# Two channels in one table product: 40 rows by 66 columns, with tables split by the channel's parity

## The chip, the cores and the metric

The kernel runs on one core of a Trainium2 chip. The metric is the device time of one execution in microseconds (us), the span of the core. A program is executed several times, and medians are quoted with the lowest and highest.

## The reference, cut to what matters

The result has two halves that are independent. The first is a local dilated attention (projection, logits, softmax, weighted sum, output projection). The second is a long convolution whose kernel K is made from 192 complex modes for each of 640 channels:

```python
logdA = dt * A
P = jnp.exp(logdA[:, :, None] * l[None, None, :])        # 640 channels, 192 modes, 2048 positions
K = jnp.einsum("dn,dnl,dn->dl", Cc, P, dB).real           # the kernel of the convolution
...
Yf = Uf * Kf                                              # convolution by FFT
y = irfft(Yf)[..., :L] + u * Dskip
```

The change touches only how K is made.

## The kernel before

The powers of a position l = a + 8 b are a product of two powers, so K of one channel is a matrix product over the modes: a table X (20 values of a) by a table Y (33 values of b). Five groups of 128 channels are worked through. The tables have modes on the partitions and keep the channels innermost, so that VectorE can make a table of many channels with one instruction:

```python
self.X = tp.tile([128, 20, 2, CW], bf16, name="Xtab", tag="Xtab", bufs=2)   # CW = 192 columns
self.Y = tp.tile([128, NB, 2, CW], bf16, name="Ytab", tag="Ytab")           # NB = 33
```

The price is that TensorE reads one channel's operands with a stride of 2 x 192 x 2 = 768 bytes: a round of four products takes 69 ns. One channel takes four small matmuls (real and imaginary part, 128 and 64 modes), and four channels g lie side by side in the four 32-column tiles of the array:

```python
for part in range(4):
    for i in range(8):
        for g in range(4):
            o = ps[32 * g:32 * g + 20, i, :]
            if part < 2:
                col = 32 * g + t0 + i
                MM(o, lhsT=X[:, :, part, col], rhs=Y[:, :, part, col], start=False, stop=False,
                   tile_position=(0, 32 * g), skip_group_check=True)
            else:
                ...          # the same with 64 rows, X[hb:hb + 64, ...]
nc.scalar.copy(out=Kd[:, q // 2, :, 8 * (q % 2):8 * (q % 2) + 8], in_=ps[:].rearrange("p t b -> p b t"))
```

Then `spread` multiplies the result Kd by 0/1 matrices that put each position where the FFT wants it. The order of the instructions of each engine is written down in the kernel as a text (`kgen00:129` means 129 matmuls of the first piece of the first table product), and the engines keep to it.

The softmax here doesn't subtract the row's maximum and nothing guards it: scores larger than these inputs give would overflow.

Of the kernel before, what the change touches and what calls it, by code (L numbers as in the profile page):

```python
# [17 lines left out]
NCH = 5  # L18
# [30 lines left out]
def sel_consts_np():  # L49
# [9 lines left out]
    def add(Wm):  # L59
        full = np.zeros((128, 32), np.float32)  # L60
        for g in range(4):
            full[32 * g:32 * g + 32, 8 * g:8 * g + 8] = Wm
        for i, m in enumerate(mats):
            if np.array_equal(m, full):
                return i
        mats.append(full)
        return len(mats) - 1
# [24 lines left out]
    return np.stack(mats, 1), plan  # L92
# [35 lines left out]
def att_consts_np():  # L128
# [11 lines left out]
prep:30 weights:15 k0:2 weights:15 k0:2 weights:15 k0:5 weights:15 k0:16 q0:25 v0:25 k1:25 q1:25 v1:25 k2:25 q2:16 kgen00:129 q2:9 kgen01 kgen02  # L140
kgen03:129 kgen02:128 kgen01:128 v2:25 k3:10 logits0:4 k3:2 logits0:4 k3:6 logits0:4 k3:7 q3:10 logits0:8 q3:15 logits0:4 v3:10 kgen10:33 kgen11:33
kgen12 kgen13:129 logits0:4 kgen10:64 logits0:8 v3:4 logits0:4 v3:6 kgen10:32 v3:5 logits0:4 kgen11:96 kgen12:96 av0:32 kgen12:32 av0:48 u0:8 av0:5
u0:2 av0:8 u0:2 av0:9 u0:2 av0:9 u0:2 av0:17 spec:20 av0 spec:12 av0:31 spec:32 out0:4 spec out0:3 spec:31 logits1:4 out0:2 spec out0 spec:16 out0:2
spec:15 out0:3 logits1:2 u1:8 logits1:2 out0:2 u1:2 out0:2 u1:2 out0 u1:2 logits1:4 u1:2 out0:2 spread0:8 out0:2 spread0:8 logits1:2 spread0:20
logits1:2 out0 logits1:4 spread0:8 logits1:4 out0:2 spread0:4 out0:2 spread0:2 out0 spread0:2 logits1:4 spec0:32 logits1:4 spec0 out0:4 spec0:16
out0:3 spec0:16 out0:2 spec0:15 out0 spec0:48 inv0:57 kgen20:129 inv0:7 logits1:8 kgen21 kgen22 kgen23:33 u2:2 logits1:2 kgen23:32 u2:2 logits1:2
kgen23:64 u2:2 kgen22:32 u2:2 kgen22:32 u2:4 kgen22:64 u2:4 kgen21:128 spread1:36 av1:6 spread1:8 av1:5 spread1:2 av1:8 spread1:2 av1:9 spread1:2
av1:9 spread1:2 av1:27 spec1:49 av1:15 spec1:16 av1 spec1:63 inv1:64 kgen30 kgen31:33 kgen30:32 kgen31:96 kgen30:96 kgen32 kgen33 u3:2 kgen33:32 u3:2
kgen33:32 u3:2 kgen33:32 u3:4 kgen33:32 kgen32:32 u3:6 kgen32:32 spread2:16 kgen32:32 spread2:20 kgen32:32 av1:21 spread2:8 av1:5 spread2:2 av1:8
spread2:4 av1:2 spread2:2 av1:12 spec2:6 logits2:4 spec2:26 av1:8 spec2 av1:19 spec2:16 av1:5 logits2:4 spec2:31 out1:2 logits2:4 spec2 out1:2  # L150
spec2:16 out1 spec2:15 out1:2 spec2 out1:3 spec2:15 out1:20 inv2:32 out1:7 inv2:25 kgen40:33 inv2:5 logits2:4 inv2:2 out1:2 kgen40:96 logits2:4 out1
logits2:4 kgen41 kgen42 kgen43 u4:2 kgen43:64 u4:2 kgen43:32 u4:2 kgen43:32 logits2:6 u4:2 logits2:2 u4:2 logits2:4 kgen42:32 u4:4 logits2:4 kgen42:32
u4:2 spread3:8 logits2:2 kgen42:32 spread3:8 logits2:2 spread3:12 kgen42:32 spread3:8 kgen41:32 spread3:6 kgen41:32 spread3:2 kgen41:32 spread3:6
av2:15 spread3:2 av2:33 kgen41:32 spec3:32 av2:8 spec3 av2:8 spec3:95 av2:43 inv3:32 av2:21 inv3:25 spread4:16 inv3:4 spread4:12 inv3 spread4:8 inv3:2
av2:16 spread4:16 av2:16 spec4:32 logits3:4 out2:2 spec4 logits3:2 spec4:16 logits3:2 out2:2 spec4:16 logits3:4 spec4:15 out2 spec4 logits3:4 spec4:16
out2:2 spec4:15 logits3:4 spec4 out2:2 spec4:15 logits3:4 out2:20 inv4:32 out2 logits3:4 out2:5 inv4:25 last00:18 inv4:7 logits3:12 out2:5 last01
logits3:2 last01:8 logits3:2 last01 last02 last01:8 last02:17 last03 av3:32 last03:9 last04 last03:8 av3:17 last04:17 av3:37 last05 av3:39 last05:17
av3:35 last06:10 out3:10 last06:8 out3:10 last07 out3:10 last07:17 last10:34 last11:17 out3:10 last11:17 last12:34 last13:34
""",
    mybir.EngineType.Activation: """  # L160
prep:11 am0:2 prep am0:9 weights:2 gens0:13 weights gens0:4 weights gens0:4 k0 gens0 mag0:3 k0 mag0:3 k0 mag0:2 k0 mag0:3 k0 mag0:2 q0 mag0:3 am1:11
gens1:5 q0:3 gens1 q0 v0:3 gens1 v0:2 gens1:2 k1:2 gens1 k1 gens1 k1 gens1 k1 gens1 q1 gens1 q1 gens1 q1 gens1 q1 gens1 q1 v1 gens1:2 v1 gens1 v1
gens1 v1:2 k2:2 gens1:2 k2:2 mag1:5 k2 mag1:3 q2:2 mag1:8 q2 kgen00 q2:2 kgen03 kgen02 kgen01 v2:5 k3:5 q3:5 mag2:16 kgen13 v3:2 logits0:2 v3:2 kgen10
v3 logits0:2 kgen11 kgen12 av0:2 u0:8 av0:2 spec:4 av0:2 spec:4 out0 spec:4 out0 spec:4 out0 u1:7 spread0:4 u1 out0 spread0:8 out0:2 spec0:6 out0
spec0:10 mag3:14 inv0:4 mag3:2 inv0:3 out0 kgen20 inv0 logits1:2 u2:2 logits1:2 kgen23 u2:4 kgen22 u2:2 kgen21 spread1:12 av1:2 spec1:16 mag4:8 inv1:7
mag4 inv1 mag4:7 kgen31 kgen30 u3:5 kgen33 u3:3 spread2:4 kgen32 spread2:8 av1:2 spec2:6 av1 spec2:4 av1 spec2:4 out1 spec2:2 out1:5 inv2:4 out1
inv2:4 kgen40 out1 u4:3 kgen43 u4:4 logits2:2 u4 spread3:2 logits2 spread3 logits2 spread3 kgen42 spread3:8 kgen41 spec3:16 av2:2 inv3:4 av2:2 inv3:3
spread4:4 inv3 spread4:8 av2:2 spec4:10 out2 spec4:6 out2:3 inv4:2 out2 inv4:2 out2:2 inv4:3 last00:2 inv4 logits3:2 out2 last01 logits3:2 last01
last02:2 av3:2 last03:2 av3:2 last04:2 av3:2 out3 last05:2 out3:3 last06:2 last07:2 out3:4 last10:2 last11:2 last12:2 last13:2
""",  # L170
    mybir.EngineType.DVE: """
prep:11 gens0 prep gens0:2 prep:2 gens0:2 genm0 gens0:2 genm0 gens0:2 genm0 gens0:2 genm0 gens0:2 genm0 gens0:2 genm0 gens0:2 genm0 gens0:2 genm0
gens0:2 genm0 gens0 weights genm0 ypos0 genm0 weights:10 xtab0 weights xtab0 gens1 xtab0:2 gens1 xtab0:2 gens1 xtab0:2 gens1 xtab0:2 u xtab0:8 gens1
genm1 xtab0 genm1 xtab0 gens1 xtab0:2 genm1 xtab0:4 gens1 xtab0:4 gens1 xtab0:2 gens1 ypos0 genm1 gens1:2 ypos0 gens1 genm1 gens1 ypos0 gens1 genm1
gens1 ypos0 gens1 genm1 gens1 ypos0 genm1 gens1:2 ypos0 gens1 genm1 gens1 ypos0 genm1 yneg0 gens1 yneg0 ypos0:2 genm1 ypos0:2 u yneg0:2 xtab1:22 u
xtab1:4 logits0 xtab1:4 logits0 xtab1:2 logits0 ypos1:2 logits0 ypos1:2 logits0 ypos1:2 logits0 ypos1:4 yneg1 ypos1:2 yneg1:2 u xtab2:2 yneg1 xtab2:2
logits0 xtab2:2 logits0 xtab2:2 logits0 xtab2:2 logits0 xtab2:8 logits0 xtab2 av0:8 xtab2 av0:2 xtab2 ypos2 xtab2 logits1 xtab2:4 logits1 xtab2:4
logits1 xtab2:2 logits1 ypos2 logits1 ypos2:2 logits1 ypos2:2 logits1 ypos2:2 logits1 ypos2 xtab3 ypos2 yneg2 ypos2:2 yneg2 xtab3 yneg2 prod0 xtab3
prod0:2 xtab3 prod0 xtab3:2 yneg2 xtab3:2 logits1 xtab3:2 logits1 xtab3:10 logits1 xtab3:2 av1 xtab3:4 av1 xtab3:4 av1 xtab3:2 ypos3:4 av1 ypos3:2
xtab4 ypos3:2 av1 ypos3:2 yneg3 ypos3:2 yneg3 xtab4 prod1 xtab4 prod1:2 xtab4 prod1 xtab4:2 yneg3 xtab4:2 yneg3 xtab4:2 av1 xtab4:2 av1 xtab4:2 av1  # L180
xtab4:18 av1:2 ypos4:2 logits2 ypos4:4 logits2 ypos4:2 logits2 yneg4 ypos4 yneg4 ypos4 prod2 ypos4 prod2:2 ypos4 prod2 yneg4 logits2 yneg4 logits2:7
av2:7 prod3:3 av2 prod3 av2 ud1 ud4 ud0 ud2 ud3 av2 logits3:6 prod4:3 logits3 prod4 logits3:4 av3:10
""",
    mybir.EngineType.Pool: """
load ypos0 load:6 prep:18 load:7 ypos0 u:13 load2:4 u ypos1:2 kgen03:4 u:6 logits0:7 ypos2:2 kgen13:4 ypos3:2 kgen23:4 ypos4:2 kgen33:4 hb kgen43:4
hb:3
""",
    mybir.EngineType.SP: """
prep:12 load:15 weights k0 weights genm1:2 q0 genm1 v0 genm1:2 k1 genm1:3 q1 genm1:2 v1 genm1 k2 tab1 fetchv0:8 fetch0:2 q2 fetch0 taby1:5 v2 tab2
fetch0:2 k3 fetch1 q3 fetch1:2 v3 u0 load2 taby2:2 fetchv1:4 taby2:3 u1 fetchv1:4 out0 fetch1 swap0:2 tab3 u2 fetch1 out0 fetch2:2 out0:2 fetch2 swap1  # L190
inv0 swap1 u3 taby3:3 tab4 taby3:2 fetchv2:4 swap2:2 inv1 u4 taby4:5 fetchv2:4 fetch2 out1:3 fetch2 swap3:2 inv2 fetch3 out1 fetch3:2 last00:3
last01:3 fetchv3:4 ud swap4:2 fetchv3:4 fetch3:2 out2:3 last02:3 last00:4 out2 last03:3 last04:3 last01 last02:4 last01 last05:3 last06:3 last01:2
last03:4 last07:3 last04:4 last05:4 out3:2 last06:4 last07:2 out3 last07:2 out3 last10:4 last11:4 last12:4 last13:4
""",
}


# [116 lines left out]
class Tables:  # L314
# [58 lines left out]
    def kgen(self, at):  # L373
# [3 lines left out]
        for q in range(4):  # L377
            with at(f"kgen{self.c}{q}"):
                self.kgen_part(q, Kd)
# [568 lines left out]
```

## Time and profile before

415.84 us was the median of three executions (415.64 to 416.18).

| engine | busy us | share of the span |
|---|---|---|
| TensorE (PE) | 316.8 | 76% |
| VectorE (DVE) | 307.1 | 74% |
| ScalarE (ACT) | 262.1 | 63% |
| table product alone (on PE) | 29.7 + 27.4 = 57.1 | 14% |

No engine is full, but two are busy for three quarters of the time, and they take turns. The prediction shows the lines on the product. Two more things of the profile before turn out to matter. The first is the row of TensorE's granted clock, in tenths of full speed, in 40 slices of 10.4 us:

```profile
PEclk9999959999759999589979696779999988799996
```

The mean clock is 0.889. The clock's records in this trace hold two values, 1.00 and 0.50, so 2 x (1 - 0.889) x 415.1 = 92 us lie at half clock (94 us by the records). Only 22 of them lie where a table product runs, counted in stretches of 2 us that hold at least one product; in the rest TensorE is idle for about half of the time. The second is how long VectorE waits for TensorE. These are groups of its instructions (busy us, mean ns, then idle us before them and what ended it):

```profile
L562 DVE TENSOR_TENSOR prod<-qk 128x2048 bf16<-128x2048 bf16 x40 | 48.2, 1225 | 11.6 <-PE ps_l L566 8.9 <-DMA qk<-qkd 2.6
L592 DVE TENSOR_TENSOR p<-vb,attn 128x2048 bf16<-128x2048 bf16 x40 | 47.4, 1224 | 12.1 <-PE ps_o L598 12.0
```

VectorE's products of the attention wait 8.9 and 12.0 us for TensorE to free their buffers.

### The profile page before, as it was taken

The page shows a single profiled execution, that of the slowest core. Times are in us where ns is not written, and L with a number is a line of the kernel's source. Part 1 is how long each engine was busy: PE and PEld are TensorE (multiplying, and loading weights), DVE is VectorE, ACT ScalarE, POOL GpSimd, SP SyncE. Part 2 cuts the span into 40 slices and gives each one's busy share as a digit, 9 for nine tenths or more (in the row PEclk, how much of TensorE's full clock was granted, in tenths as well). Part 3 has the DMA queues.
Part 4 walks back from the last instruction along what each step waited for, and adds up shares of the span by engine and source line. Part 5 has one row for each costly group of instructions (what it writes and reads, how often), then busy time and mean ns, then how long its engine had stood idle before and what let it go on. Part 6 is the DMA issues. An engine that isn't in the chain of part 4 may idle for free. (4 is left out here: it accounts for less than half of the span.)

```text
span 415.1 us, 13105 instructions
## 1 busy us (share of the span) xinstructions
PE 316.8 (76%) x5645; PEld 196.1 (47%) x5654; DVE 307.1 (74%) x445; ACT 262.1 (63%) x570; POOL 50.4 (12%) x101
## 2 busy tenths in 40 slices
PE   0569249989359988799788886799999875897781
PEld 0224114335233355356476556565666663475561
DVE  0558978995974999589999599959972765786500
ACT  0587977987004533489976596469747977573552
POOL 7453300004014010200000200011000400000000
PEclk9999959999759999589979696779999988799996
DMA  5999765668998847869308530727166499616656
GB/s 75 217 212 178 202 164 190 214 216 260 207 213 205 271 126 171 233 146 254 114 17 230 154 86 2 205 64 154 51 195 209 138 369 313 137 49 177 160 134 95
DMA packets 78841, 70.67 MB, mean 170 GB/s; under 512 B 35264, under 2 KB 73904, under 8 KB 76992
## 3 DMA queue, kind: packets, MB, share of 16 engines
q1 hardware_dynamic: 71616, 54.96, 51.3%
q0 software_dynamic: 4144, 12.18, 11.9%
q10 hardware_dynamic: 3024, 2.70, 2.9%
q8 instruction: 44, 0.72, 0.7%
q14 instruction: 13, 0.11, 0.1%
HBM read 37.82 MB, written 23.65 MB: 148 GB/s over the span
## 5 line engine op out<-in xcount | busy, mean ns | idle before, releaser
L515 PE MATMUL ps_p<-xT,w 128*128 128x512 bf16 x291 | 76.4, 409 | 20.9 <-ACT st L516 15.4
L515 PEld LDWEIGHTS <-w 128*128 128x128 bf16 x300 | 30.0, 103 | 60.3 <-issue 33.3
L562 DVE TENSOR_TENSOR prod<-qk 128x2048 bf16<-128x2048 bf16 x40 | 48.2, 1225 | 11.6 <-PE ps_l L566 8.9
L592 DVE TENSOR_TENSOR p<-vb,attn 128x2048 bf16<-128x2048 bf16 x40 | 47.4, 1224 | 12.1 <-PE ps_o L598 12.0
L438 ACT CAST A<-ps_f 128x512 bf16<-128x512 f32 x80 | 42.8, 613 | 19.0 <-PE ps_f L437 18.6
L516 ACT CAST st<-ps_p 128x512 bf16<-128x512 f32 x60 | 34.6, 586 | 23.1 <-PE ps_p L515 21.1
L456 ACT CAST Sp<-ps_f 128x512 bf16<-128x512 f32 (+1 forms) x96 | 42.4, 564 | 4.6 <-PE ps_f L452 3.5
L398 PE MATMUL ps_k<-Ytab,Xtab 128*20 128x33 bf16 x1280 | 29.7, 248 | 15.1 <-issue 15.1
L598 PE MATMUL ps_o<-p,cHs 64*32 64x256 bf16 x640 | 27.7, 297 | 12.5 <-DVE p L592 7.7
L452 PE MATMUL ps_f<-A,cT 64*128 64x128 bf16 (+1 forms) x768 | 29.4, 211 | 5.4 <-ACT Sp L456 3.5
L398 PEld LDWEIGHTS <-Xtab 128*20 128x20 bf16 x1280 | 23.3, 128 | 21.6 <-issue 20.2
L405 ACT CAST Kd<-ps_k 128x264 bf16<-128x264 f32 x20 | 7.6, 380 | 40.7 <-PE ps_k L403 40.5
L479 PE MATMUL ps_ia<-cE,Sp 128*128 128x128 bf16 x160 | 25.5, 254 | 8.0 <-DVE Sp L467 7.8
L452 PEld LDWEIGHTS <-cT 64*128 64x128 bf16 x768 | 21.7, 96 | 18.4 <-issue 17.1
L403 PE MATMUL ps_k<-Ytab,Xtab 64*20 64x33 bf16 x1280 | 27.4, 244 | 3.5 <-issue 3.5
L611 PE MATMUL ps_op<-wo,oT 128*128 128x320 bf16 x160 | 29.0, 301 | 0.7 <-ACT ob L612 0.6
L480 ACT CAST Z<-ps_ia 128x512 bf16<-128x512 f32 x40 | 22.4, 604 | 10.7 <-PE ps_ia L479 8.3
L403 PEld LDWEIGHTS <-Xtab 64*20 64x20 bf16 x1280 | 22.4, 123 | 8.0 <-issue 6.7
L479 PE MATMUL ps_ia<-cE,UT 128*128 128x128 bf16 x160 | 25.4, 253 | 0.0
L306 DVE TENSOR_TENSOR Xtab<-Xtab,Xg 128x768 bf16<-128x768 bf16 (+2 forms) x35 | 24.5, 699 | 0.3
L307 DVE TENSOR_TENSOR krtmp<-Xtab,Xg 128x768 bf16<-128x768 bf16 (+2 forms) x35 | 24.4, 698 | 0.0
L345 ACT ACTIVATE mag<-ta 128x192 bf16<-128x192 f32 x80 | 22.6, 397 | 1.2 <-DVE Ytab L351 1.2
(109 smaller groups left out, 571.0 us busy)
## 6 DMA issues: line engine op xcount, KB each, us to landing
qk<-qkd SPq DMA_DIRECT2D x20, 263.0 KB, 5.3
qkd<-st SPq DMA_DIRECT2D x8, 640.0 KB, 5.3
UT<-Sp SPq DMA_DIRECT2D x10, 512.0 KB, 6.7
Gdram<-cs SPq DMA_DIRECT2D x11, 384.0 KB, 3.0
HB<-k_HB POOLq DMA_DIRECT2D x4, 1024.0 KB, 16.1
vb<-vd SPq DMA_DIRECT2D x16, 196.5 KB, 5.0
Xg<-Gdram SPq DMA_DIRECT2D x4, 768.0 KB, 7.7
Zdram<-Z SPq DMA_DIRECT2D x3, 1024.0 KB, 8.6
```

Of the source, the lines that this page charges most:

```text
L398: MM(o, lhsT=X[:, :, part, col], rhs=Y[:, :, part, col], start=False, stop=False, tile_position=(0, 32 * g), skip_group_check=True)
L403: MM(o, lhsT=X[hb:hb + 64, :, part - 2, col], rhs=Y[hb:hb + 64, :, part - 2, col], start=False, stop=(part == 3), tile_position=(hb, 32 * ...
L438: nc.scalar.copy(out=A1[:].rearrange("p k r s t -> p (k r) s t")[:, :, sig, 8 * q:8 * q + 8], in_=ps[:])
L452: nc.tensor.matmul(ps[h][:, kk], lhsT=C["T"][hs, k, 64 * (1 - r):64 * (1 - r) + 128], rhs=A1[hs, k, r, s0:s1, :].rearrange("p s t -> p (s ...
L456: nc.scalar.copy(out=o, in_=ps[h][:].rearrange("p k (s t) -> p s t k", t=64))
L479: nc.tensor.matmul(ps[:, i], lhsT=X[:, h, 4 * t:4 * t + 4, :].rearrange("p g k -> p (g k)"), rhs=C["E"][:, n_, :], start=(i == 0 and n_ == ...
L515: nc.tensor.matmul(ps[:], lhsT=self.w[which][:, kt, 128 * ct:128 * ct + 128], rhs=self.xT[:, kt, 512 * sc:512 * sc + 512], start=(kt == 0) ...
L516: nc.scalar.copy(out=st[:, ct], in_=ps[:])
L562: V.tensor_tensor(out=pr[:], in0=self.qk[b][ct][:, 0, HALO:].unsqueeze(1).to_broadcast([128, 4, PB]), in1=windows(self.qk[b][ct][:, 1, 8 - ...
L592: V.tensor_tensor(out=p2[:], in0=windows(self.v[b][t][:, 2 * qp:2 * qp + 2, 0:PH], 2, 4), in1=at[:].unsqueeze(2).to_broadcast([128, 4, 2, ...
L598: nc.tensor.matmul(ps[half][32 * q:32 * q + 32, t % 2], lhsT=C["Hs"][r], rhs=p2[r, m, q2, :], start=(t % 2 == 0 and m == 0), stop=(m == 3) ...
L611: nc.tensor.matmul(ps[:], lhsT=oT[:, t, 128 * s:128 * s + 128], rhs=self.wo_sb[:, t, 320 * eh:320 * eh + 320], start=(t == 0), stop=(t == 4))
```

## The change

The intent: half as many table products, each larger. Two channels s = 0, 1 are put in one product, 40 rows (s, a) by 66 columns (s, b). The two diagonal blocks are the result, and the other two are thrown away by 0/1 matrices that are split by s, so `spread` has twice as many matmuls. The tables keep channels in an order "even g first, then odd g" (halves of 96 columns), which takes three more complex products on VectorE. The text of the order is made anew. The core of the diff:

```diff
-        self.X = tp.tile([128, 20, 2, CW], bf16, name="Xtab", tag="Xtab", bufs=2)
+        self.X = tp.tile([128, 2, 20, 2, HW_], bf16, name="Xtab", tag="Xtab", bufs=2)
...
-            for i in range(8):
-                for g in range(4):
-                    o = ps[32 * g:32 * g + 20, i, :]
-                    ...
+            for j in range(n):
+                t = 16 * h + t0 + j
+                for gg in range(2):
+                    r, m = (slice(64 * gg, 64 * gg + 64), 64 + t) if part > 1 else (slice(0, 128), 32 * gg + t)
+                    MM(ps[64 * gg:64 * gg + 40, j, :], lhsT=X[r, :, :, part % 2, m].rearrange("p s a -> p (s a)"),
+                       rhs=steps(Y[r, 0, part % 2, m:], [HW_, 2], [2 * CW, NB]), ...)
...
 (spread)
+                for s in range(2):
+                    b0 = NB * s + 8 * bhi
...
+                    nc.tensor.matmul(o, lhsT=C["SEL"][:, 2 * wi + s, :], rhs=k, ..., stop=(s == 1), ...)
-            U = fp.tile([128, 2, 64, 16], bf16, name="U", tag="U", bufs=1)
+            U = fp.tile([128, 2, 64, 16], bf16, name="U", tag="UK", bufs=1)
```

(Cut: the order of the channels in the transposes at the start, which the text calls flips, the 0/1 matrices, the three small copies that were moved to make room in memory, and the new text of the order.)

## The prediction

> **What bounds the kernel now.** I read the page first (busy shares and groups), then TensorE's timeline, the busy times by stretches, the forms of VectorE's groups and at last the chain that ended last.
>
> ```profile
> PE 316.8 (76%) x5645; PEld 196.1 (47%) x5654; DVE 307.1 (74%) x445; ACT 262.1 (63%) x570; POOL 50.4 (12%) x101
> L398 PE MATMUL ps_k<-Ytab,Xtab 128*20 128x33 bf16 x1280 | 29.7, 248 | 15.1 <-issue 15.1
> L403 PE MATMUL ps_k<-Ytab,Xtab 64*20 64x33 bf16 x1280 | 27.4, 244 | 3.5 <-issue 3.5
> q8 instruction: 44, 0.72, 0.7%
> ```
>
> No engine is full. The table product is 2560 of 5654 matmuls, 57.1 us busy, and 18.6 us of idle time stand before it with no releaser ("issue"). The instruction queue brought 44 pieces of 16 KB, about one for each 256 instructions of TensorE. Such a gap lies inside a run of products that all have their data:
>
> ```profile
> 106.44 1.07 PE L398 MATMUL ps_k<-Ytab,Xtab 128*20 128x33 bf16 x51
> 113.54 0.44 PE L398 MATMUL ps_k<-Ytab,Xtab 128*20 128x33 bf16 x13 [6.03 <-issue]
> ...
> 307.93 1.28 PE L398 MATMUL ps_k<-Ytab,Xtab 128*20 128x33 bf16 x64
> ...
> 313.27 0.22 PE L398 MATMUL ps_k<-Ytab,Xtab 128*20 128x33 bf16 x1
> ```
>
> Columns are start, length, what. I read the 6.03 us as a late piece of instructions: one landed at about 111.9 us. The third line gives the product's real pace: 64 products are 16 rounds of four (one per column tile), (1.28 - 0.25) / 15 = 69 ns a round. The single records agree: four start within some 10 ns, then nothing for about 60 ns. So it isn't the issue of eight instructions that sets 69 ns[...]. The last line is one product alone, whose weights were loaded 0.2 us before: 218 ns. Contiguous matmuls of 64, 96 and 128 columns last 193, 206 and 219 ns, a straight line that gives 180 for 33 columns. Hence even alone, 33 columns that lie 768 bytes apart cost 38 ns more than contiguous ones.
>
> Where TensorE has room:
>
> ```profile
> 100.00:110.00 10.00, 6.28 (x214) 4.44 (x204) 7.42 (x18) 1.94 (x4) 1.69 (x3) 0.90 1.04 272
> 110.00:120.00 10.00, 2.64 (x128) 2.25 (x128) 7.00 (x12) 0.38 (x1) 0.00 (x0) 0.50 1.16 220
> ...
> 210.00:220.00 10.00, 10.00 (x237) 8.62 (x236) 9.93 (x19) 7.45 (x18) 0.00 (x0) 0.81 0.21 62
> ...
> 300.00:310.00 10.00, 9.80 (x277) 6.89 (x279) 9.04 (x9) 4.18 (x9) 0.00 (x0) 1.00 0.58 151
> 310.00:320.00 10.00, 9.74 (x260) 6.04 (x252) 1.28 (x2) 7.09 (x15) 0.00 (x0) 1.00 0.82 268
> ```
>
> (stretch, then busy us of TensorE, weight loads, VectorE, ScalarE, GpSimd, then clock, DMA share, GB/s.) Only around the first table does TensorE stand idle; around the third and fifth it is full. The five products run at about 98-122, 141-170, 214-236, 258-280 and 301-326 us.
>
> ```profile
> 349.42 3.41 DVE uD L886 x3
> 352.83 1.15 DVE p L592
> 353.98 0.04 issue
> 354.02 1.04 PE ps_o L598 x15
> ```
>
> The last chain begins with VectorE's work on uD, whose 2.5 MB transfer goes into memory freed after the last product. So a later product pushes the whole tail.
>
> [...]in the last stage 64-column matmuls start every 29 ns. [...]the pace is also 69 ns at half clock, so it isn't the array's. [...]here the next kind of matmul starts 165 ns after the last product, about 95 more than its 69.
>
> **The change part by part.**
> Table product. 1280 instead of 2560, each 40 rows (so a 64-column tile) by 66 columns; half the result is thrown away. Rounds: before 2560 / 4 = 640, after 1280 / 2 = 640. Before: 640 x 69 = 44 us. If the cost is per strided column, a round of 66 columns takes up to 2 x 69 = 138 ns; by the lone product, 166 + 2 x 52 leaves about 104 of reading, 121 with the same rest of 17. I take 130: 640 x 130 = 83 us, **+39 us**. Weight loads double too (40 strided columns; 20 last 111-123 ns where 32 contiguous last 92), and stay below that.
> Fetch gaps. At 65 ns per product, 256 instructions last 8 us instead of 2.2, so pieces arrive in time. I give back 15 of 18.6 us: **-15 us**, most of it at the first table (1.1 + 6.0 + 4.4).
> Spread. Each 0/1 product twice: 36 more per channel group, 28 of 256 and 8 of 128 columns, four tiles side by side: 7 x 107 + 2 x 53 = 0.86 us, five times: **+4 us**.
> Pieces. The order breaks the product into 107 pieces, not 81: 26 x 0.1 = **+2.5 us**[...]. The flips make 30 more small matmuls at the start: +1 us.
> TensorE in all: 39 - 15 + 4 + 2.5 + 1 = about **+31 us**.
> VectorE. The table goes from 8 to 11 complex products, 32 to 44 instructions, of the same elements; a multiply of 384 elements lasts 355 ns and of 768 556 ns, so some 155 is fixed, of which about 85 overlaps the next. 60 x 0.07 = +4 us.
> ScalarE. Copies of 264 columns (380 ns) x20 become 20 of 396 (488, as the 384-column copies of the end) and 10 of 264: 13.6 - 7.6 = +6 us. It has room.
> Shared U/K buffer, Dskip's load, zeros from DRAM: some tens of us lie between K's last read and the next U's need, and a U lands in 3.9 us. I count 0.
>
> From TensorE to the end. First table: +7.8 + 0.9 - 11 = about -2, TensorE being what that stage waits for. The other four: 7.8 + 0.9 + 0.5 less 1 to 4 of gaps, +5 to +8 each, together +26. Of it, TensorE's waits for VectorE's spectrum products near 206 and 249 us (3.5 and 4.2 us) can take in some 6, other small waits some 5, and the new order may regain a few. 26 - 2 - 11 - 4 = +9; without the last two +18.
>
> **The rivals.**
> 1. The product is bound by its count, not by its columns (the change's own idea). Then 640 x 35 = 22 us, -22 - 15 + 7 = -30 on TensorE, of which half reaches the end: 395 to 405. For it: the eight instructions of a round are 8.6 ns each, and the fetch gaps are real. Against it: the bursts of four, the 218 ns of a lone product, and the 64x32 matmuls of the attention, 16 instructions in 109 ns.
> 2. A round has a fixed time whatever its size[...]. Then 640 x 69 stays, TensorE gets -15 + 7, and the time falls by 3 to 10: 406 to 413. For it: I have only one width of strided columns. Against: a lone product and its load are nearly as slow as four at once.
> 3. The columns cost double, but VectorE, at 9 or more tenths in most slices of the middle, sets the end and TensorE's excess goes into its waits: 416 to 421.
>
> **Range and chances.** My sum lies at +9 to +18 for the main case, to which I give some six in ten; the rivals pull down, 138 ns a round pulls up to +25. A change with so much work around it is likelier one that was meant to pay, which keeps a quarter for faster. I say 425 us, range 401 to 442; faster by over 2% (below 407.5) 0.26, within 2% 0.19, slower (above 424.2) 0.55.
>
> **What would show it.** Right: runs of 12 products start at 120 to 138 ns a round, mean duration of one about 310 ns, ps_k busy well over 80 us, "issue" before it under 5 us, and TensorE's share rising. Wrong: rounds near 69 or 35 ns, ps_k busy under 60. If rounds are 130 and the time still falls, then the order or the fetch gaps were worth more than I gave. A wait of U's load or of K's copies (the shared buffer) would be a cost that I left out.

## The result and the profile after

| | median us | lowest to highest | executions |
|---|---|---|---|
| before | 416.01 | 415.64 to 419.93 | 4 |
| after | 452.63 | 450.60 to 457.01 | 4 |

The ratio is 1.087 (95% interval 1.077 to 1.098): slower. Ratios here and below are the mean time of one kernel's fast runs over that of the other's of the same rounds, so not quite the ratio of the medians. With one core, "fast" only means within 1.5% of the fastest execution of the same kernel on that chip.

The page of the kernel after: busy shares, the clock's row and the instruction queue.

```profile
PE 374.0 (83%) x4594; PEld 238.8 (53%) x4594; DVE 311.2 (69%) x505; ACT 266.3 (59%) x580; POOL 49.8 (11%) x100
PEclk9999789996879655699875698558987996999996
q8 instruction: 36, 0.59, 0.6%
```

TensorE has 1060 matmuls and as many weight loads fewer than before (by the PEld counts, as some matmul records of before are missing) and is busy 57.2 us longer. VectorE's and ScalarE's busy times rose by 4.1 and 4.2 us, about as predicted (+4 and +6). The clock's row has far more dips: the mean is 0.844 in this execution and 0.823 to 0.844 in all four, which makes 142 us at half clock by the records, 48 us more. 86 of them lie in stretches with products (22 before). Eight instruction pieces fewer were brought.

The groups that answer to those shown of before, and the zero matmuls that clear the product's accumulators:

```profile
L428 PE MATMUL ps_k<-Ytab,Xtab 128*40 128x66 bf16 (+1 forms) x1280 | 92.6, 304 | 0.0
L422 PE MATMUL ps_k<-Ytab,zw 128*128 128x396 bf16 (+1 forms) x30 | 10.0, 413 | 3.5 <-DVE Ytab L383 3.5
L587 DVE TENSOR_TENSOR prod<-qk 128x2048 bf16<-128x2048 bf16 x40 | 48.0, 1224 | 30.7 <-PE ps_l L591 28.2 <-DMA qk<-qkd 2.3 <-PE ps_o L623 0.2
L617 DVE TENSOR_TENSOR p<-vb,attn 128x2048 bf16<-128x2048 bf16 x40 | 47.6, 1223 | 24.9 <-PE ps_o L623 24.8
```

The product takes 92.6 us for half the count. Its idle time "issue" fell from 18.6 us to nothing. VectorE now waits 28.2 and 24.8 us for TensorE, 32 us more than before: there TensorE sets the pace.

TensorE's timeline in the second product (start, length, what):

```profile
161.35 3.07 PE L428 MATMUL ps_k<-Ytab,Xtab 128*40 128x66 bf16 x44
...
187.19 0.91 PE L428 MATMUL ps_k<-Ytab,Xtab 64*40 64x66 bf16 x12
```

44 products are 22 rounds of two column tiles: (3.07 - 0.30) / 21 = 132 ns a round, where 0.30 is the length of one product. The products of 64 rows go a little faster, (0.91 - 0.30) / 5 = 122 ns. The starts of all products in the trace have a median of 127 ns a round, at full and at half clock alike. Before, a round of four took 69 ns.

The busy times by stretches (columns as in the prediction; the clock is the third number from the end) show the products of the second, third and fourth group of channels, and one stretch without a product for comparison:

```profile
170.00:180.00 10.00, 10.00 (x143) 7.97 (x143) 9.18 (x20) 1.66 (x4) 0.00 (x0) 0.50 0.59 217
210.00:220.00 10.00, 7.04 (x142) 4.05 (x136) 7.52 (x15) 10.00 (x26) 0.00 (x0) 1.00 0.31 94
240.00:250.00 10.00, 10.00 (x108) 6.60 (x106) 6.00 (x19) 4.40 (x8) 0.00 (x0) 0.50 0.01 2
290.00:300.00 10.00, 10.00 (x107) 6.83 (x105) 1.31 (x6) 4.30 (x8) 0.00 (x0) 0.50 0.63 185
```

In the three with a product TensorE is busy for 10.00 of 10 us, at a clock of 0.50; in the one without, for 7.04 us at 1.00. Other matmuls that run at half clock slow down with it: the projections' start every 427 ns there and every 216 ns at full clock.

Where the 34.7 us between the two profiled spans (415.1 and 449.8) came from, by the pages: the product's busy time 92.6 - 57.1 = +35.5; all other matmuls (374.0 - 92.6) - (316.8 - 57.1) = +21.7; TensorE's idle time (449.8 - 374.0) - (415.1 - 316.8) = -22.5, of which 18.6 are the vanished instruction gaps. The sum is +34.7. (The two product groups of before overlap by 1.3 us. Counted once, the product gives +36.8 and the other matmuls +20.4.)

### The profile page after: what moved, and what is told of

It reads as the page before. It is cut to its first block, busy times and chain, and to the rows that moved or that the text cites.

```text
span 449.8 us, 11064 instructions
## 1 busy us (share of the span) xinstructions
PE 374.0 (83%) x4594; PEld 238.8 (53%) x4594; DVE 311.2 (69%) x505; ACT 266.3 (59%) x580; POOL 49.8 (11%) x100
## 5 line engine op out<-in xcount | busy, mean ns | idle before, releaser
L540 PE MATMUL ps_p<-xT,w 128*128 128x512 bf16 x300 | 81.0, 424 | 23.5 <-ACT st L541 20.8
L428 PE MATMUL ps_k<-Ytab,Xtab 128*40 128x66 bf16 (+1 forms) x1280 | 92.6, 304 | 0.0
L428 PEld LDWEIGHTS <-Xtab 128*40 128x40 bf16 (+1 forms) x1280 | 75.5, 158 | 21.0 <-issue 20.6
L587 DVE TENSOR_TENSOR prod<-qk 128x2048 bf16<-128x2048 bf16 x40 | 48.0, 1224 | 30.7 <-PE ps_l L591 28.2
L617 DVE TENSOR_TENSOR p<-vb,attn 128x2048 bf16<-128x2048 bf16 x40 | 47.6, 1223 | 24.9 <-PE ps_o L623 24.8
L430 ACT CAST Kd<-ps_k 128x396 bf16<-128x396 f32 (+1 forms) x30 | 13.8, 459 | 65.1 <-PE ps_k L428 65.1
L478 PE MATMUL ps_f<-A,cT 64*128 64x128 bf16 (+1 forms) x768 | 28.2, 208 | 8.4 <-ACT A L464 4.4
L623 PE MATMUL ps_o<-p,cHs 64*32 64x256 bf16 x640 | 29.5, 309 | 5.3 <-ACT oT L627 2.8
L505 PE MATMUL ps_ia<-cE,Sp 128*128 128x128 bf16 x160 | 24.8, 251 | 6.5 <-DVE Sp L493 3.6
L636 PE MATMUL ps_op<-wo,oT 128*128 128x320 bf16 x160 | 27.1, 300 | 2.5 <-ACT oT L627 1.4
L340 DVE TENSOR_TENSOR Xtab<-Xtab,Xg 128x384 bf16<-128x384 bf16 (+2 forms) x50 | 26.7, 535 | 0.1
L341 DVE TENSOR_TENSOR krtmp<-Xtab,Xg 128x384 bf16<-128x384 bf16 (+2 forms) x50 | 26.8, 535 | 0.0
L377 ACT ACTIVATE mag<-ta 128x192 bf16<-128x192 f32 x80 | 22.3, 380 | 4.6 <-DVE Ytab L383 4.6
L591 PE MATMUL ps_l<-prod,cGs 128*32 128x512 bf16 x160 | 23.8, 414 | 1.3 <-DVE prod L587 1.3
L505 PE MATMUL ps_ia<-cE,UT 128*128 128x128 bf16 x160 | 24.8, 251 | 0.0
L505 PEld LDWEIGHTS <-Sp 128*128 128x128 bf16 x160 | 18.3, 115 | 8.3 <-issue 7.9
```

The costliest lines, as they stand in the source:

```text
L428: MM(ps[64 * gg:64 * gg + 40, j, :], lhsT=X[r, :, :, part % 2, m].rearrange("p s a -> p (s a)"), rhs=steps(Y[r, 0, part % 2, m:], [HW_, 2] ...
L478: nc.tensor.matmul(ps[h][:, kk], lhsT=C["T"][hs, k, 64 * (1 - r):64 * (1 - r) + 128], rhs=A1[hs, k, r, s0:s1, :].rearrange("p s t -> p (s ...
L505: nc.tensor.matmul(ps[:, i], lhsT=X[:, h, 4 * t:4 * t + 4, :].rearrange("p g k -> p (g k)"), rhs=C["E"][:, n_, :], start=(i == 0 and n_ == ...
L540: nc.tensor.matmul(ps[:], lhsT=self.w[which][:, kt, 128 * ct:128 * ct + 128], rhs=self.xT[:, kt, 512 * sc:512 * sc + 512], start=(kt == 0) ...
L587: V.tensor_tensor(out=pr[:], in0=self.qk[b][ct][:, 0, HALO:].unsqueeze(1).to_broadcast([128, 4, PB]), in1=windows(self.qk[b][ct][:, 1, 8 - ...
L591: nc.tensor.matmul(ps[mp][r:r + 32], lhsT=C["Gs"][:, ct, :], rhs=pr[:, 2 * mp:2 * mp + 2, PH * half:PH * half + PH], start=(ct == 0), stop ...
```

## The experiments

My theory after reading the traces: the product's pace is set by how many separate places in memory its two operands are read from, and this slow reading also lets the clock fall, so that other matmuls slow down. The rivals were that the pace comes with the shape (two tiles instead of four, 40 rows, 66 columns), that the rest of the change (flips, spread, order) carries much of the loss, and that the clock plays no part. All kernels below are timed; where it isn't said otherwise they are edits of the kernel after. Those that read other table entries compute a wrong K. The first four ran together on one chip, the next four on another; pairs_right and pairs_dense ran together, and the last two by themselves.

| run | median us (range) | before on that chip, median | ratio [95%] | product busy us | PE busy us | us at half clock (of it in stretches with products) |
|---|---|---|---|---|---|---|
| before | 416.0 | | | 57.1 | 316.8 | 94 (22 of 106) |
| after | 452.6 (450.6-457.0) | 416.0 | 1.087 [1.077, 1.098] | 92.6 | 374.0 | 142 (86 of 134) |
| both_dense | 387.8 (385.9-391.3) | 422.0 | 0.931 [0.908, 0.953] | 31.6 | 298.3 | 53 (5 of 72) |
| moving_dense | 406.3 (404.2-409.1) | 422.0 | 0.973 [0.957, 0.989] | 57.2 | 323.3 | 57 (11 of 94) |
| weights_dense | 443.1 (435.5-445.3) | 422.0 | too few fast runs | 83.1 | 355.4 | 99 (56 of 126) |
| one_channel | 428.4 (420.4-429.8) | 422.0 | too few fast runs | 62.6 | 335.4 | 91 (33 of 114) |
| long_dense | 430.3 (430.1-430.9) | 420.9 | 1.039 [1.037, 1.042] | 84.4 | 348.9 | 51 (3 of 120) |
| spread_light | 452.6 (451.9-452.8) | 420.9 | 1.093 [1.090, 1.096] | 92.6 | 371.9 | 151 (90 of 138) |
| before_dense | 417.7 (416.3-419.7) | 420.9 | 1.009 [1.000, 1.018] | 32.7 | 299.6 | 115 (28 of 90) |
| moving_pairs | 410.3 (404.9-412.6) | 420.9 | 0.987 [0.968, 1.005] | 60.3 | 331.7 | 74 (21 of 100) |
| pairs_right | 411.8 (408.2-416.3) | 416.8 | 0.996 [0.986, 1.006] | 60.1 | 330.8 | 60 (12 of 102) |
| pairs_dense | 557.9 (555.1-559.4) | 416.8 | 1.350 [1.340, 1.361] | 47.7 | 336.9 | 219 (6 of 86) |
| pairs_dense_rows | 461.5 (457.5-469.1) | 416.8 | 1.118 [1.108, 1.127] | 47.7 | 336.7 | 116 (7 of 88) |
| pairs_order | 423.8 (417.7-427.1) | 421.9 | 1.012 [0.989, 1.035] | 60.3 | 334.9 | 74 (19 of 102) |

(Busy times and half clock are those of the one profiled execution of each kernel; those of one_channel and moving_pairs count as slow executions. The medians take in slow executions too: of the kernel before, 5 of 7 on the first two chips and 7 or 8 of 11 on the others; of weights_dense and one_channel, 3 of 4. The ratios leave them out. The two fast executions of the kernel before on the first chip took 414.6 and 420.8 us, so a ratio's last per cent means little.)

### both_dense, moving_dense, weights_dense: which operand, and whether the stride

Counts, shapes, tiles and order of the kernel after stay. Only the addresses change: the 40 weights, the 66 columns, or both are read from neighbouring elements.

```diff
-  lhsT=X[r, :, :, part % 2, m].rearrange("p s a -> p (s a)"), rhs=steps(Y[r, 0, part % 2, m:], [HW_, 2], [2 * CW, NB])
+  lhsT=steps(X[r, 0, 0, 0, 0:], [1, 40]),                     rhs=steps(Y[r, 0, 0, 0:], [1, 2 * NB])   # both_dense
   # moving_dense changes rhs alone, weights_dense lhsT alone
```

> The changed kernel, its table products reading 40 and 66 neighbouring columns (wrong result on purpose, same counts, sizes, tiles and waits). Theory (cost per strided column): a round of two products falls from 115-131 ns to 30-45 ns, TensorE loses some 55 us, and the time falls from 452 to 400-418 us. Rival (the slowdown is the rest of the change: new order, doubled spread, more VectorE instructions, shared U/K buffer): the time stays at 440-455 us whatever the round does.

> Only the moving operand reads neighbouring columns; the 40 weight columns stay strided. If the moving operand sets the round, as I predicted, a round falls to the weights' own 80-100 ns and the time to 425-442 us. If the weight load sets it, the round stays at 115-131 ns and the time at 448-455 us.

> Only the weights read neighbouring columns; the 66 moving columns stay strided. If the moving operand sets the round: 110-131 ns stay and the time falls by less than 6 us (446-453 us). If the weight load sets it, the round falls to 75-100 ns and the time to 425-442 us.

The product's group in the three, in this order:

```profile
L428 PE MATMUL ps_k<-Ytab,Xtab 128*40 128x66 bf16 (+1 forms) x1280 | 31.6, 195 | 1.6 <-issue 1.6
```

```profile
L428 PE MATMUL ps_k<-Ytab,Xtab 128*40 128x66 bf16 (+1 forms) x1280 | 57.2, 238 | 0.0
```

```profile
L428 PE MATMUL ps_k<-Ytab,Xtab 128*40 128x66 bf16 (+1 forms) x1280 | 83.1, 287 | 0.0
```

The same 1280 matmuls take 31.6 us when both operands are dense. The median rounds are 29 ns (both dense), 70 ns (40 strided weights) and 113 ns (66 strided columns): 70 / 40 = 1.75 ns for each strided weight column, 113 / 66 = 1.71 ns for each strided moving column. With both strided it is 127 ns, above the larger of the two and far below their sum. So the shape isn't the cause. With dense operands, and nothing charged for making them dense, the change would have paid: a ratio of 0.931 to the kernel before. None of the three times fell where it was expected: 388 us lies below the range, moving_dense's 406 far below its own, and weights_dense's one fast execution took 435.5, 10 us under its range.

### one_channel: the rest of the change with the old products

Each product of the kernel after becomes two of 20 by 33 in 32-column tiles, as before; flips, tables, spread, shared buffer and order are those of the kernel after.

```diff
-  for gg in range(2):
-      MM(ps[64 * gg:64 * gg + 40, j, :], lhsT=X[r, :, :, part % 2, m]..., rhs=steps(Y[r, 0, part % 2, m:], [HW_, 2], [2 * CW, NB]), ...)
+  for g in range(4):
+      gg, s = g // 2, g % 2
+      MM(ps[32 * g:32 * g + 20, j, NB * s:NB * s + NB], lhsT=X[r, s, :, part % 2, m], rhs=Y[r, :, part % 2, HW_ * s + m], ...)
```

> The changed kernel with the product of the kernel before: four products of 20 rows by 33 columns in the place of each two of 40 by 66, in its place in the order (wrong result on purpose, the rest as changed). Theory: rounds of four at 69 ns, ps_k about 44 us of rounds instead of 80, part of the fetch gaps back (5-15 us), time 420-432 us. Rival (the rest of the change costs it): time 440 us or more.

```profile
L433 PE MATMUL ps_k<-Ytab,Xtab 64*20 64x33 bf16 (+1 forms) x2560 | 62.6, 251 | 10.0 <-issue 9.9
L455 PE MATMUL ps_s<-Kd,cSEL 128*32 128x256 bf16 (+1 forms) x360 | 13.2, 295 | 0.2 <-ACT K L458 0.2
```

The one fast execution took 420.4 us; the two of the kernel before on that chip took 414.6 and 420.8. So the wide product carries most of the loss; what the rest costs in time can't be told from so few fast runs (the medians, mostly of slow executions, are 428.4 and 422.0). TensorE's other matmuls are busy 335.4 - 62.6 = 272.8 us against 259.7 before, +13 (+12 with the overlap counted once), at nearly the same time at half clock (91 and 94 us). This is read from an execution that counts as slow, and on another chip than before's. The 0/1 products account for 13.2 - 8.0 = 5 of it and the zero matmuls (30 longer ones in place of 20) for 8.6 - 4.4 = 4; the 8.0 and 4.4 are the same groups in the kernel before. It is also seen here that the new order alone leaves 9.9 of the 18.6 us of instruction gaps.

### long_dense: a product as long as the changed one, without its strides

The 40 weights are dense, and 264 dense columns stand in place of 66 strided ones, so that TensorE is occupied about as long (113 ns a round as measured, against 127 in the kernel after).

```diff
-  MM(ps[64 * gg:64 * gg + 40, j, :], lhsT=X[r, :, :, part % 2, m]..., rhs=steps(Y[r, 0, part % 2, m:], [HW_, 2], [2 * CW, NB]), ...)
+  MM(steps(ps[64 * gg:64 * gg + 40, 0, 0:], [1, 264]), lhsT=steps(X[r, 0, 0, 0, 0:], [1, 40]), rhs=steps(Y[r, 0, 0, 0:], [1, 264]), ...)
```

> The changed kernel; each product reads 40 neighbouring weight columns and 264 neighbouring moving columns (wrong result on purpose)[...]. Theory (the strided product also lets the clock fall to half, and every other matmul near it pays): half-clock time falls from 142 us to 60-90 us, and the time by the 10 us of shorter rounds and 10-15 us more, to 425-433 us. Rival (the clock has no part, the seconds go where the rounds go): 440-446 us.[...]

```profile
PE 348.9 (81%) x4585; PEld 218.5 (51%) x4594; DVE 311.1 (73%) x505; ACT 265.6 (62%) x580; POOL 49.8 (12%) x100
PEclk9999759999999779999899996999999998999996
L428 PE MATMUL ps_k<-Ytab,Xtab 128*40 128x264 bf16 (+1 forms) x1280 | 84.4, 278 | 1.2 <-DVE Ytab L385 1.1
```

The median round is 113 ns. The product is 8.2 us shorter (84.4 against 92.6), yet the median is 22.3 us lower; spread_light, a near copy of the kernel after on long_dense's own chip, took 452.6 there too. The clock's row has lost its long dips; all four executions have a mean clock of 0.943 to 0.950. The other matmuls take 348.9 - 84.4 = 264.5 us in place of 281.4: 16.9 us less, with 91 us less at half clock. A rival is that slow strided reads hold up the matmuls behind them at any clock. The traces speak for the clock: the projections' matmuls of 512 columns start every 216 ns at full and every 427 ns at half clock, in both kernels. The other matmuls' busy time that lies at half clock is 63.0 us in the kernel after, 27.2 in long_dense and 42.6 in the kernel before; if half of it is the clock's price, it cost 17.9 us against long_dense (16.9 measured) and 10.2 against before. Scaling 16.9 us to the 48 us that the kernel after has more at half clock than the kernel before gives nearly the same estimate: 16.9 x 48 / 91 = 9 us of TensorE's time. This meets the accounting: of +21.7 us for other matmuls, one_channel explains about 13 and the clock about 9.

### spread_light: the doubled 0/1 products

The second product of each pair is cut to one column; all else as in the kernel after. The rival is that the doubling is a main cost.

```diff
+                    if s == 1:
+                        o, k = o[:, 0, 0, 0:1], k[:, 0, 0, 0:1]
```

> The changed kernel; the second 0/1 product of each pair has one column in the place of 256 or 128 (wrong result on purpose). My sum gave 4 us for the doubling. Theory: the time falls by 2-6 us from the changed kernel's, to 446-451 us. Rival[...]: by over 8 us.

```profile
L452 PE MATMUL ps_s<-Kd,cSEL 128*32 128x1 bf16 (+2 forms) x360 | 9.7, 241 | 0.3 <-issue 0.2
```

A miss: the busy time of the 0/1 products fell from 13.8 to 9.7 us, and the time didn't, as far as two chips can be compared (452.6 us both, ratios 1.093 and 1.087). No gain from fewer columns is seen at the end. Their count was kept, so the cost of issuing twice as many is not tested.

### before_dense: the kernel before without strides

```diff
-  MM(o, lhsT=X[:, :, part, col], rhs=Y[:, :, part, col], ...)
+  MM(o, lhsT=steps(X[:, 0, 0, 0:], [1, 20]), rhs=steps(Y[:, 0, 0, 0:], [1, NB]), ...)      # both kinds, edits of the kernel before
```

> The kernel before, its products reading 20 and 33 neighbouring columns (wrong result on purpose). If columns set its rounds too, a round falls from 69 to 30-55 ns (eight instructions, at 6.8 ns each as in the attention's matmuls, would be 54), product rounds from 44 to 20-35 us, the fetch gaps stay or grow (18-30 us), and the time falls to 398-412 us. If a round has a fixed time, 69 ns and 415 us stay. Compared with the 388 us of the changed kernel with dense columns it tells what halving the count is worth.

```profile
L398 PE MATMUL ps_k<-Ytab,Xtab 128*20 128x33 bf16 x1280 | 16.9, 183 | 30.4 <-issue 30.4
L403 PE MATMUL ps_k<-Ytab,Xtab 64*20 64x33 bf16 x1280 | 15.8, 181 | 6.3 <-issue 6.3
```

A miss in the time: rounds of four fall from 69 to 28 ns (the median; 25 is the commonest), but the idle time "issue" doubles from 18.6 to 36.7 us, and the time stays (ratio 1.009). That these waits are for instructions shows in the DMA records: in the kernel before all seven of them over 0.3 us end 1.3 to 1.7 us after a piece of instructions landed, and eleven of twelve do here. So with dense operands the products of the kernel before wait for their instructions, 36.7 us in all. There halving the count pays: both_dense has 1.6 us of this wait and a ratio of 0.931. The change's idea was right for dense tables and wrong for these.

### moving_pairs and pairs_right: two channels side by side in memory

If the cost is for each separate place read, two neighbours should cost as one. moving_pairs reads the right number of pairs from the wrong entries; pairs_right is a whole, right kernel: the columns of Y are ordered by 2 m + s, so that a table entry of both channels is a pair of neighbours, X keeps its halves, and the generators are read in a permuted order where the two meet. The instruction counts and the order are those of the kernel after.

```diff
-  rhs=steps(Y[r, 0, part % 2, m:], [HW_, 2], [2 * CW, NB])
+  rhs=Y[r, :, part % 2, 2 * m:2 * m + 2]            # 33 pairs of neighbours
-  b0 = NB * s + 8 * bhi
+  b0 = 16 * bhi + s                                 # pairs_right: Kd's columns are now (b, s)
```

> The changed kernel; the moving operand takes its 66 columns as 33 pairs of neighbours, 768 bytes apart (wrong result on purpose, since the tables aren't laid out so). [...]the strided weights (70 ns alone) set the round at 70-90 ns and the time is 405-416 us. If the cost is per column whatever its neighbour, 115-131 ns and 450 us stay.

> The changed kernel with a right result and the two channels of a table element side by side (the moving operand is 33 pairs of neighbours; the 40 weights stay strided). [...]if that also keeps the clock up: rounds of two product matmuls at about 70 ns, as in the run with wrong pairs (now bound by the 40 strided weights), ps_k busy about 60 us, half clock 70 to 85 us, time 404 to 412, ratio to before 0.97 to 0.99. The rival, that the gain of that run came from its wrong data and not from the order in memory: rounds of 110 ns or more and a time of 430 or above. The reordered generators (read in a permuted order by ScalarE and, once a channel, by VectorE) should cost under 3 us.

The page of pairs_right:

```profile
PEclk9999959999998988999699996899989968999996
L434 PE MATMUL ps_k<-Ytab,Xtab 128*40 128x66 bf16 (+1 forms) x1280 | 60.1, 249 | 0.0
```

Rounds are 70 ns here and in moving_pairs, as with dense columns: now the 40 strided weights set them. Time at half clock falls to 60 us. The result agrees bit for bit with that of the kernels before and after when the programs' arithmetic is carried out off the chip, and on the chip it is within the reference's tolerance. The first of these is what counts: moving_pairs, one_channel and spread_light, which are wrong, are within the tolerance too. It takes 411.8 us: some 8% less than the kernel after, by the two ratios to the kernel before (0.996 and 1.087). Against the kernel before the interval contains 1, so I can't call it faster; the means of the fast runs are 411.2 and 412.9.

### pairs_dense, pairs_dense_rows: dense weights too, by copies on ScalarE

ScalarE, with 184 us free, copies X into a table where a product's 40 weights are neighbours. X is kept once in place of twice, to make room. The second kernel differs only in the order in which a copy walks: it reads with a stride and writes in a row.

```diff
+  nc.scalar.copy(out=XD[:, r, m:m + 24].rearrange("p m (s a) -> p s a m", s=2), in_=X[:, :, :, r, m:m + 24])              # pairs_dense
+  nc.scalar.copy(out=XD[:, r, m:m + 24].rearrange("p m (s a) -> p m s a", s=2), in_=X[:, :, :, r, m:m + 24].rearrange("p s a m -> p m s a"))   # _rows
```

> As pairs_right, and ScalarE copies each channel's X table into a table in which a product's 40 weights lie side by side (8 copies of 960 elements a channel, an estimated 0.9 us each from 585 ns for 512 elements: 36 us more on ScalarE, which has 184 us free in the changed kernel). [...]33 x 1.7 = 56 ns at most a round, ps_k busy about 45 to 50 us, half clock 55 to 75 us, time 395 to 404, ratio to before 0.94 to 0.97. The rival, that ScalarE's copies come in the way of the copies out of PSUM that TensorE waits for: rounds as short, but a time no better than pairs_right's (405 to 415). A second rival, that pairs of neighbours cost nearly nothing: rounds near 30 ns and a time near 390.

> pairs_dense again, with each of ScalarE's 40 copies writing its 960 elements one after the other and reading them with a stride of 384 bytes, where before it wrote with a stride of 80 bytes and took 4.57 us (4.8 ns an element). The product's rounds should stay at 57 ns[...]. If it is the strided writing that was slow: copies of 0.9 to 1.9 us, 36 to 76 us on ScalarE in all, time 398 to 412 (below pairs_right's 411.8 only if they come out near the lower end). The rival, that ScalarE pays for each strided element whichever side is strided: copies of 4 us or more and a time of 530 or above.

First pairs_dense, then pairs_dense_rows:

```profile
L413 ACT COPY Xdense<-Xtab 128x960 bf16<-128x960 bf16 x40 | 170.0, 4571 | 2.6 <-DVE Xtab L348 2.6
L440 PE MATMUL ps_k<-Ytab,Xdense 128*40 128x66 bf16 (+1 forms) x1280 | 47.7, 232 | 0.3 <-issue 0.3
```

```profile
L413 ACT COPY Xdense<-Xtab 128x960 bf16<-128x960 bf16 x40 | 72.0, 1883 | 2.6 <-DVE Xtab L348 2.6
L552 PE MATMUL ps_p<-xT,w 128*128 128x512 bf16 x300 | 84.5, 437 | 37.7 <-ACT st L553 35.2 <-DMA xT<-in_A_x_dram 2.5
```

On TensorE they did what they should: rounds of 58 ns, 58 / 33 = 1.76 ns a pair. This settles that the cost is by pair and not by column (66 x 1.71 would be 113). My estimate of 0.9 us a copy was wrong, because it came from a copy with contiguous elements (585 ns for 512 of them). It took 4.57 us when writing with a stride of 80 bytes (4.8 ns an element) and 1.88 us when reading with one of 384 bytes (2.0 ns). TensorE then waits for ScalarE's copies out of PSUM (35.2 us before the projections in the second one's trace), and both kernels lose.

### pairs_order: two idle stretches of TensorE moved

pairs_right shows TensorE idle for 10.7 us where ScalarE stood in eight exponentials (6.32 us) and a table load (1.28 us):

```profile
58.89 5.48 PE L546 MATMUL ps_p<-xT,w 128*128 128x512 bf16 x17 [10.68 <-ACT st L547]
```

I put four copies between the exponentials, used the time gained for projections that had come later, and had the second table's negative half made at once.

```diff
 (ScalarE's order)
-am1:8 gens1:5 v0:5 gens1 k1 ...
+am1:2 v0 am1:2 v0 am1:2 v0 am1:2 v0 gens1:2 v0 gens1:2 k1 ...
 (TensorE's)
-q2:15 kgen00:13 kgen01:13 kgen00:36 kgen01:36 q2:5 ...
+q2:20 v2:20 kgen00:13 kgen01:13 kgen00:36 kgen01:36 v2:5 ...
 (VectorE's)
-yneg1 ypos1:2 logits0 yneg1 xtab2:2 av0 ... xtab2:2 yneg1 xtab2:2 yneg1
+yneg1 ypos1:2 yneg1:3 logits0 xtab2:2 av0 ...
```

> pairs_right with another order near two of TensorE's longest idle stretches, which its trace shows: 10.7 us at 48 us, where TensorE waits for copies out of PSUM that stand behind eight exponentials and a table load on ScalarE, and 4.5 us at 150 us, where the second product waits for the table's negative half, which VectorE makes after other work. Four copies go between the exponentials, the projections that followed the first product go before and into it, and the negative half is made at once. If these waits are on the path: 3 to 10 us less than pairs_right, 402 to 409, ratio to before 0.97 to 0.98, which would beat both kernels. The rival, that VectorE (313 us busy, nine tenths and more in most slices of the middle) sets the end there: the idle time moves to later waits for VectorE and the time stays at 409 to 414.

```profile
157.02 0.39 PE L630 MATMUL ps_o<-p,cHs 64*32 64x256 bf16 x1 [9.87 <-DVE p L624]
```

A miss. The wait at 48 us is down to 2.2 us, and one of 9.87 us for VectorE has appeared at 147 us. With more projections ahead of it the first product started at 105.2 in place of 97.7 us. VectorE then waited 9.8 us, not 4.4, for matmuls of the logits that stand behind that product, and came to the next table 7.4 us later. The time isn't shown to be better or worse than the kernel before (ratio 1.012, interval 0.989 to 1.035; median 423.8 against 421.9, mostly slow executions). Three orders were changed at once, so which of them did it isn't tested. No version here is shown to beat the kernel before by 2% with a right result.

## Why the prediction was wrong, point by point

The direction ("slower", to which I had given 0.55) and the cost of a strided column held. The time did not: 452.6 against 425, and above the upper end of 442.

**Product, "640 x 130 = 83 us, +39 us".** Right. The median round is 127 ns, and the busy time rose by 35.5 us. "The cost is per strided column" is shown by the four runs with dense or paired operands, with one correction: it is per separate place, as two neighbours cost like one, and the weights pay too (1.75 ns each). I had counted the weights as hidden; alone they would set 70 ns, and beside 66 strided columns they add 14 (127 against 113). So that 130 came so near is partly luck: it was picked between 121 and 138, and the columns alone give 113.

**Fetch gaps, -15.** Measured -18.6. About half of it is owed to the new order, not to the wider product, since one_channel keeps 9.9 us.

**Spread +4, pieces +2.5, flips +1.** Other matmuls took 13 us more even with the old products. 5 are the 0/1 products and 4 the zero matmuls, which I had left out. In spread_light no gain from fewer columns of the former is seen. Counted in the traces, runs of products of one kind went from 66 to 78, not from 81 to 107.

**VectorE +4, ScalarE +6, shared buffers 0.** +4.1 and +4.2 by the pages. No wait for the shared buffer stood among the larger ones of the profile; I didn't test it by itself.

**TensorE in all, "+31 us".** The measured counterpart is 35.5 - 18.6 + 21.7 = +38.6. The term that was missing is the clock: 48 us more at half clock, an estimated 9 us on the other matmuls. I had noted that the product's pace is the same at half clock and left the clock out of the sum. It doesn't matter for the product (127 ns a round at half clock, 128 at full), but it does for the work mixed in with it (216 and 427 ns from one of the projections' matmuls to the next).

**"From TensorE to the end": the step that failed.** I let waits take up 6 to 11 us of TensorE's excess and the new order up to 4, and so left +9 to +18 of the +31. Some 7 us had been lost before that by a slip: the sum by tables, 26 - 2 = 24, takes back 11 us of instruction gaps at the first table and some 10 at the others, more than the 15 of the sum by parts or the 18.6 that there were. Measured, 38.6 became 34.7: under 4 us were taken up, not the 13 to 22 between +31 and my result. Some waits did shrink as I said (TensorE's for VectorE's spectrum products from 7.8 to 3.6 us, its waits for the attention's products from 7.7 to 2.2). But others grew: for ScalarE's copies of the projections from 15.4 to 20.8, for the table's negative half from 0.9 to 3.5. And VectorE, whose waits for TensorE in the attention grew by 32 us, was no longer ahead. In this ring of engines that wait for each other's buffers, work added to one delayed the others' next inputs; the idle time before it wasn't a reserve. That is the reading of the two traces; no run tests it by itself. pairs_order, where a wait of 10.7 us was taken away and one of 9.9 us came in its place, is in line with it.

**The rivals.** Rival 1 (bound by count) fell for strided tables and holds for dense ones (before_dense and both_dense). Rival 2 (a fixed time a round) fell: 29, 58, 70, 113 and 127 ns were all had with the same count. Rival 3 (VectorE absorbs) fell, as its waits for TensorE more than doubled.

**What stays open** is what makes the clock fall. It isn't idleness alone: in the stretches with products of the kernel after TensorE was busy for 85 of the 86 us at half clock. And a stride isn't needed: before_dense has none in its products and spends 115 us there, though with gaps. These are the moving columns in a nanosecond, over all tiles, worked out from the rounds, with the share of the product stretches at half clock behind each: after 2 x 66 / 127 = 1.04 (64%), weights_dense 1.17 (44%), one_channel and before 4 x 33 / 72 = 1.83 and 4 x 33 / 69 = 1.91 (29 and 21%), moving_dense, moving_pairs and pairs_right 1.89 (12, 21 and 12%), pairs_dense 2.28 (7%), both_dense 4.6 and long_dense 4.7 (7 and 3%). before_dense, whose bursts of 4 x 33 / 28 = 4.7 alternate with gaps, has 31%, and the runs near 1.9 scatter from 12 to 29%. No run varied the rate alone, so that it decides is not shown.

## What to carry to other kernels

Before making matmuls fewer and larger, compare the pace of a round with columns and with instructions; if the operands are strided, count the separate places that both are read from, and put what belongs together side by side in memory first (here, with dense weights, 66 columns took 113 ns a round one by one and 58 ns in pairs). Read the clock's row together with the busy shares: here a slow stream (127 ns a round) on a full TensorE (10.00 of 10 us) went with a clock of 0.50, which its neighbours paid, by an estimated 9 us. And don't count idle time of an engine as a reserve for its own added work unless the view shows that what ends the wait would still come at the same time (here under 4 of 38.6 us were taken up).
